# A planned instruction list for RWKV attention and a two-layer PReLU product: another way to pick the list, small reciprocals for the tables of powers, and idle matmuls ahead of the first dense product

## The chip, the core and the metric

The kernel runs on one core of one Trainium2 chip. The metric is device time in microseconds (us), the median of the runs shown. In what follows PE is TensorE (PEld its weight loads), DVE is VectorE, ACT is ScalarE, POOL is GpSimd and SP is SyncE, which only issues DMA transfers here.

## What is computed

A recurrent attention with a state of 48 x 48 per head runs over 768 steps, for 4 batches and 8 heads; its result goes through two dense products with a PReLU between them.

```python
def _attn_ref(r, k, v, w, u):            # (4, 8, 768, 48), w and u (8, 48)
    state = np.zeros((B, H, D, D))
    for t in range(S):
        kt, vt, rt = (k[:, :, t], v[:, :, t], r[:, :, t])
        cur = np.einsum('bhd,bhe->bhde', u[None] * kt, vt)
        y[:, :, t] = np.einsum('bhd,bhde->bhe', rt, state + cur)
        state = w[None, :, :, None] * state + np.einsum('bhd,bhe->bhde', kt, vt)

def _moe_ref(x, w_in, w_out, alpha):     # x (3072, 384), w_in (384, 2048)
    h = x @ w_in
    g = np.maximum(h, 0.0) + alpha * np.minimum(h, 0.0)
    return g @ w_out
```

`w` lies between 0.85 and 0.95.

## The kernel before

The 768 steps are cut into six chunks `c` of 128, and the eight heads into four pairs `q`. For a chunk and a pair, `attention` scales r by powers of w (`raw<-raw,W`, L403) and k by their inverses, forms the scores A (L459, or L469 in chunk 0), adds a diagonal `cu` and masks them (`base`, L479 to L505), and multiplies by v (`out`, L531; `out_of_tokens`, L561). In chunk 0 the diagonal comes from `c_sum` (L418), four tiny matmuls on the product r times k (L411), each followed by an idle one. The result is split into a rounded part and a rest (`split`, L626 to L637), the pieces `xh` and `xl` of the dense input; small transfers `lower` (`x<-x`, L367) bring the rows of pair 0 into place. The state T is updated by k^T v (`state_product`, L585, and `state_of_tokens`, L574). For pair 3 of chunk 0 k is first scaled by `scale_k` on DVE (`kk<-kk,wtok`, L592).

`table(m)` makes, per pair, the powers of w from -64 to 64 (`W`): a scan gives the upper half (L297), and a reciprocal of 64 columns the lower half (L300).

The dense part has 16 slices `i` of 128 hidden columns per chunk. `m_in` (L860, in later chunks L813) forms hp, ACT and DVE form the rounded `gh` and the rest `gl` of the PReLU, and `m_out` (L902) adds to three accumulators. Each operand is a sum of two rounded parts, so three matmuls stand for one. The parts `wh` and `wl` of slice i are made once, by `weights`: a load of 768 KB (`wraw<-wall`, L323), then ACT (L345), DVE (L348), ACT (L352) and DVE (L355). `wh_87` and `wl_103` are the parts of slice 0, `wh_88` and `wl_104` those of slice 1, and so on; in the changed kernel all these numbers are one higher.

Every operation is recorded as a `Piece` with an engine, an assumed duration and its dependences. `Plan.in_order` plans the pieces twelve times, forward with urgencies and backward for new ones (`forward`, `backward`), keeps the list whose planned end is earliest, and the program is written in the order of its planned starts. Each engine then runs its own part of the list strictly in order. So this one list sets the order on PE, DVE, ACT, POOL and SP. SP has eight transfers in flight at most. Where the plan has a gap on PE before the first `m_out`, the program writes idle matmuls (`warm`, L986: 128x256 on a tile `busy` of zeros) into it; 26 more stand at the very start.

Of the kernel before, what the change touches and what calls it, by code (L numbers as in the profile page):

```python
# [2 lines left out]

# [13 lines left out]
AF = mybir.ActivationFunctionType  # L17
ALU = mybir.AluOpType
# [9 lines left out]
MLAG = 3  # L28
# [9 lines left out]
DMA_RATE = 275.0  # L38

OVERLAP = {"DVE": 0.08, "ACT": 0.1}  # L40
ROUNDS = 12


class Buf:
# [31 lines left out]
class Plan:  # L76
# [1 line left out]


    def __init__(self):  # L80
        self.pieces, self.groups, self.log = [], {}, {}

    def buf(self, make, group=None, bufs=0):
        b = Buf(make, group, bufs)
# [4 lines left out]
    def add(self, eng, us, fn, r=(), w=(), rank=0.0, kb=0.0):  # L89
        p = Piece(eng, us, fn, r, w, rank, kb)  # L90
        for ref, wr in p.uses:
            b, part = ref if isinstance(ref, tuple) else (ref, None)
            if isinstance(b, Half):
                b, part = b.buf, (b.j, part)
            log = self.log.setdefault(b, [])
            for other, opart, owr in log:
                if other is not p and ((wr or owr) and (part is None or opart is None or part == opart)
                                       or b.bank and other.eng != p.eng and "PE" not in (other.eng, p.eng)):
                    p.after.add(other)
            log.append((p, part, wr))  # L100
        self.pieces.append(p)
        return p

    def in_order(self):
        for bs in self.groups.values():
            bs[:] = [b for b in bs if b in self.log]
            for n, b in enumerate(bs):
                users = [p for p, _, _ in self.log[b]]
                for p in users:
                    if n >= b.bufs:  # L110
                        p.after.update(q for q, _, _ in self.log[bs[n - b.bufs]])
                    if n:
                        p.behind.add(self.log[bs[n - 1]][0][0])
                    p.behind.add(users[0])
        number = {p: i for i, p in enumerate(self.pieces)}
        for p in self.pieces:
            p.behind.discard(p)
        best = None
        urgency = {p: p.rank for p in self.pieces}
        for n in range(ROUNDS):  # L120
            order = self.forward(urgency, number)
            end = max(p.end for p in order)
            if best is None or end < best[0]:
                best = end, {p: (p.start, p.end) for p in order}
            urgency = self.backward(number)
        for p, (start, end) in best[1].items():
            p.start, p.end = start, end
        return sorted(self.pieces, key=lambda p: (p.start, number[p]))

    def run(self, need, ready, key):  # L130

# [26 lines left out]
    def forward(self, urgency, number):  # L158
        def ready(p):
            return max([q.end + q.lag + (0.0 if q.eng == p.eng else 0.2 if q.eng == "PE" else 0.1) for q in p.after]  # L160
                       + [q.start + 0.001 for q in p.behind] + [0.0])

        dma, done = 0.0, []
        for p, start in self.run({p: p.after | p.behind for p in self.pieces}, ready,
                                 lambda p: (urgency[p], number[p])):
            p.start, p.end = start, start + p.us
            if p.eng == "SP":
                dma = max(dma, p.end + 1.5) + p.kb / DMA_RATE
                p.end = dma + 0.5
                self.landed.append(p.end)  # L170
            done.append(p)
        return done

    def backward(self, number):

        heirs, followers = {p: set() for p in self.pieces}, {p: set() for p in self.pieces}
        for p in self.pieces:
            for q in p.after:
                heirs[q].add(p)
            for q in p.behind:  # L180
                followers[q].add(p)
        ends, starts, dma = {}, {}, 0.0

        def ready(p):
            t = [starts[q] + p.lag + p.early + (0.0 if q.eng == p.eng else 0.2 if p.eng == "PE" else 0.1) for q in heirs[p]]
            t += [starts[q] + 0.001 - p.us for q in followers[p]]
            t = max(t + [0.0])
            return max(t, dma) + 1.8 + p.kb / DMA_RATE if p.eng == "SP" else t

        was = {p: p.start + p.us for p in self.pieces}  # L190
# [10 lines left out]
def rwkv_prelu_kernel(ctx: ExitStack, tc, rk, vkr, wP, uP, u, wall, alpha, w, r_all, k_all, v_all, oT):  # L201
    nc = tc.nc
# [7 lines left out]
    P = H // 2  # L210
    NB, NM = C * P, C * NF
    plan = Plan()
    add = plan.add
# [26 lines left out]
    T = [fixed([112, B, D], f"T{m}") for m in range(P)]  # L240

    uw = fixed([112, P, 2], "uw")
    wh, wl = ([fixed([128, 2 * NK, 128], f"{n}{i}", F32R) for i in range(NF)] for n in ("wh", "wl"))
    flag = fixed([1, 1], "flag", I32)
    busy = fixed([128, 256], "busy", mybir.dt.bfloat16)
# [9 lines left out]
    for t, dram in ((wp, wP), (up, uP)):  # L255
# [7 lines left out]
        rank=-100)  # L263
# [3 lines left out]
        r=[ones], w=[ident], rank=-100)  # L267
# [3 lines left out]
        w=[ones], rank=-100)  # L271
# [19 lines left out]
    for g in range(2):  # L291
        add("POOL", 0.25, lambda g=g: nc.gpsimd.tensor_tensor(
            out=uw()[half(g), :, g], in0=up()[half(g)], in1=wp()[half(g)], op=ALU.mult),
            r=[up, wp], w=[uw], rank=-97)
    def table(m):
        t, a = W[m], wp
        add("DVE", 0.3, lambda: nc.vector.tensor_tensor_scan(  # L297
            out=t()[:, 64:129], data0=a()[:, m:m + 1].broadcast_to([112, 65]), data1=unit(), initial=0.0,
            op0=ALU.mult, op1=ALU.add), r=[wp, unit], w=[t], rank=10 * m - 95)
        add("DVE", 0.55, lambda: nc.vector.reciprocal(t()[:, 0:64], t()[:, 128:64:-1]), w=[t], rank=10 * m - 95)  # L300
        add("POOL", 0.55, lambda: nc.gpsimd.tensor_tensor(
            out=w128()[:, m:m + 1], in0=t()[:, 128:129], in1=t()[:, 128:129], op=ALU.mult), r=[t], w=[(w128, m)],
            rank=10 * m - 85)
# [880 lines left out]
```

## Time and profile before

| | us |
|---|---|
| three runs | 491.72, 491.02, 489.53 (median 491.02) |
| the profiled execution | 490.89 |
| its span, first to last instruction | 489.0 |
| PE busy | 479.3 (98%) |
| DVE busy | 364.1 (74%) |
| ACT busy | 245.7 (50%) |
| POOL busy | 73.0 (15%) |

The profiled execution's own time is 1.89 us more than its span. In a busy time the ends of matmuls are modelled, so a busy PE is one that has been given work, not one at its peak; idle matmuls count as busy.

### The profile page before, as it was taken

How to read it: one execution, taken by the hardware profiler on the slowest of the kernel's cores; microseconds unless marked ns; L12 is line 12 of the kernel's file. 1: busy time of each engine (PE TensorE's matmuls, PEld its weight loads, DVE VectorE, ACT ScalarE, POOL GpSimd, SP SyncE). 2: the span in 40 equal slices, each digit the busy share in tenths (PEclk: the TensorE clock that was granted, in tenths of full speed). 3: DMA queues.
4: the chain of work that ended last, by engine and by line, in shares of the span. 5: the costliest groups of instructions: out<-in, count | busy, mean ns of one | idle time of the engine just before them, and what ended most of it. 6: DMA issues, size and time to landing. Idle time of an engine off the chain costs nothing.

```text
span 489.0 us, 10992 instructions
## 1 busy us (share of the span) xinstructions
PE 479.3 (98%) x4431; PEld 397.0 (81%) x4431; DVE 364.1 (74%) x658; ACT 245.7 (50%) x579; POOL 73.0 (15%) x76
## 2 busy tenths in 40 slices
PE   9999999999999999999999999999999999999996
PEld 7767877888888887887888888887888888888885
DVE  6989999899967897887897686686785745445542
ACT  1786776666654454543455554343753323532322
POOL 7416040041010132210210121030000000000000
PEclk9999999999999999999999999999999999999999
DMA  8894779640232633441122341120220000100001
GB/s 241 269 296 136 250 182 277 214 153 2 97 115 75 200 86 100 137 104 52 52 87 87 118 104 52 36 87 1 71 67 1 1 0 1 64 1 0 2 1 70
DMA packets 24600, 47.58 MB, mean 97 GB/s; under 512 B 3552, under 2 KB 12256, under 8 KB 24544
## 3 DMA queue, kind: packets, MB, share of 16 engines
q1 hardware_dynamic: 24000, 46.55, 31.5%
q8 instruction: 37, 0.61, 0.5%
q10 hardware_dynamic: 544, 0.27, 0.2%
q14 instruction: 19, 0.16, 0.1%
HBM read 38.15 MB, written 6.29 MB: 91 GB/s over the span
## 4 chain that ended last, share of the span: by engine, by line
PE 87%; ACT 5%; DVE 4%; DMA 1%; issue 1%; POOL 0%; SPq 0%; DVEq 0%; ACTq 0%
PE acc L902 36%; PE hp L860 19%; PE hp L813 18%; PE A L459 3%; PE y L539 2%; PE y L561 2%; PE hp L986 2%; ACT x L626 2%; DMA x<-x 1%; PE A L902 1%; PE hp L561 1%; ACT base L491 1%; PE y L574 1%; ACT g L825 1%; PE hp L574 1%
## 5 line engine op out<-in xcount | busy, mean ns | idle before, releaser
L860 PE MATMUL hp<-x,wh 128*128 128x512 f32 x288 | 98.3, 398 | 1.0 <-PE y L634 0.8
L902 PE MATMUL acc<-gh,wh 128*128 128x512 f32 (+1 forms) x282 | 79.8, 391 | 1.0 <-ACT gh L849 1.0
L902 PE MATMUL acc<-gh,wl 128*128 128x512 f32 (+1 forms) x282 | 79.7, 390 | 0.0
L902 PE MATMUL acc<-gl,wh 128*128 128x512 f32 (+1 forms) x282 | 79.2, 389 | 0.0
L844 DVE TENSOR_TENSOR g<-hp,g 128x512 f32<-128x512 f32 x48 | 32.7, 688 | 58.6 <-PE hp L813 30.7
L860 PEld LDWEIGHTS hp<-x,wh 128*128 128x128 f32 x288 | 54.0, 188 | 14.4 <-PE y L634 1.1
L849 ACT ACTIVATE gh<-g 128x512 fp32r<-128x512 f32 x48 | 30.2, 632 | 70.7 <-DVE g L846 62.2
L813 PE MATMUL hp<-x,wh 128*128 128x256 f32 (+1 forms) x192 | 62.4, 347 | 0.0
L825 ACT ACTIVATE g<-hp 128x256 f32<-128x256 f32 x96 | 34.4, 380 | 55.4 <-PE hp L813 55.0
L434 POOL TENSOR_TENSOR rr<-rr,kk 128x384 f32<-128x384 f32 x20 | 25.6, 1278 | 235.2 <-DMA kk<-vkr 140.7
L902 PEld LDWEIGHTS acc<-gl,wh 128*128 128x128 f32 x282 | 51.5, 188 | 10.9
L902 PEld LDWEIGHTS acc<-gh,wh 128*128 128x128 f32 x282 | 50.6, 188 | 11.7 <-ACT gh L849 1.4
L902 PEld LDWEIGHTS acc<-gh,wl 128*128 128x128 f32 x282 | 51.1, 188 | 10.6
L860 PE MATMUL hp<-x,wl 128*128 128x512 f32 x144 | 57.1, 397 | 1.0 <-issue 0.5
L867 DVE SCALAR_TENSOR_TENSOR g<-hp,alph,g 128x512 f32<-128x512 f32 x48 | 35.9, 747 | 18.5 <-ACT g L866 18.4
L866 ACT ACTIVATE g<-hp 128x512 f32<-128x512 f32 x48 | 28.6, 596 | 33.1 <-PE hp L860 32.8
L871 DVE TENSOR_TENSOR gl<-g,gh 128x512 fp32r<-128x512 f32 x48 | 36.1, 753 | 9.7 <-ACT gh L870 5.8
L813 PEld LDWEIGHTS hp<-x,wh 128*128 128x128 f32 x192 | 36.1, 188 | 7.0 <-ACT g L825 3.1
L870 ACT ACTIVATE gh<-g 128x512 fp32r<-128x512 f32 x48 | 30.1, 628 | 20.2 <-DVE g L867 18.3
L403 DVE TENSOR_TENSOR raw<-raw,W 112x512 f32<-112x512 f32 x45 | 39.5, 892 | 0.6 <-DMA raw<-rk 0.5
L491 ACT ACTIVATE base<-eye,cu 128x64 f32<-128x64 f32 x144 | 38.7, 337 | 0.8 <-DVE cu L442 0.8
L850 DVE TENSOR_TENSOR gl<-g,gh 128x512 fp32r<-128x512 f32 x48 | 32.8, 689 | 7.6 <-ACT gh L849 4.0
(184 smaller groups left out, 877.9 us busy)
## 6 DMA issues: line engine op xcount, KB each, us to landing
wraw<-wall SPq DMA_DIRECT2D x16, 767.8 KB, 5.3
raw<-rk SPq DMA_DIRECT2D x45, 224.0 KB, 3.5
v<-vkr SPq DMA_DIRECT2D x24, 192.0 KB, 4.0
kk<-vkr SPq DMA_DIRECT2D x21, 192.0 KB, 3.5
rr<-vkr SPq DMA_DIRECT2D x20, 192.0 KB, 2.5
oT<-o SPq DMA_DIRECT2D x12, 256.0 KB, 2.5
x<-x SPq DMA_DIRECT2D x36, 64.0 KB, 2.8
oT<-g SPq DMA_DIRECT2D x5, 256.0 KB, 2.3
```

The source lines that it names most:

```text
L403: add("DVE", 0.72 if c < 2 else 0.85, lambda t=t, tab=tab: nc.vector.tensor_tensor(out=t(), in0=t(), in1=tab().broadcast_to([112, B, L]), ...
L491: add("ACT", 0.39 if first else 0.34, lambda g=g, b=b: nc.scalar.activation(base[g]()[:, b], (ident if first else eye)(), AF.Copy, scale=c ...
L813: nc.tensor.matmul(bank()[:, cols], ws[a], xs[b], start=start and j == 0, stop=stop and j == 2, skip_group_check=True)
L825: add("ACT", 0.37, lambda: nc.scalar.activation(t()[:, cols], bank()[:, src], AF.Copy), r=[bank], w=[(t, part)], rank=rank - 100).early = 0.3
L844: add("DVE", 0.75, lambda g=g, bank=bank: nc.vector.tensor_tensor(out=g(), in0=bank(), in1=g(), op=ALU.add), r=[bank], w=[g], rank=m - 100)
L849: add("ACT", 0.64, lambda g=g, gh=gh: nc.scalar.activation(gh(), g(), AF.Copy), r=[g], w=[gh], rank=m - 100)
L850: add("DVE", 0.73, lambda g=g, gh=gh, gl=gl: nc.vector.tensor_tensor(out=gl(), in0=g(), in1=gh(), op=ALU.subtract), r=[g, gh], w=[gl], ran ...
L860: nc.tensor.matmul(hp(), a[i]()[:, k], x[c]()[:, k], start=(k == 0 and j == 0), stop=(k == NK - 1 and j == 2))
L867: add("DVE", 0.75, lambda: nc.vector.scalar_tensor_tensor(out=g(), in0=hp(), scalar=alph()[:, i:i + 1], in1=g(), op0=ALU.mult, op1=ALU.max ...
L870: add("ACT", 0.64, lambda: nc.scalar.activation(gh(), g(), AF.Copy), r=[g], w=[gh], rank=n - 100)
L871: add("DVE", 0.73, lambda: nc.vector.tensor_tensor(out=gl(), in0=g(), in1=gh(), op=ALU.subtract), r=[g, gh], w=[gl], rank=n - 99)
L902: nc.tensor.matmul(bank(), a[i]()[:, NK + k], x()[:, cols], start=(begin and j == 0), stop=(end and j == 2), skip_group_check=(c == C - 1))
```

## The change

There are three edits. First, `in_order` now plans from several starts: for each of five assumed delays of the loads (0 to 2 us, which `forward` adds to loads that start between 4 and 35 us), once from the ranks and once from the best list so far with random noise. Each list is then replayed in its fixed order (`replay`) with five delays, and the one whose mean end is earliest is kept; to a replayed end some us are added for each PE gap of over 0.9 us between 8 and 40 us. Second, the lower half of `W` is now the upper half times one reciprocal per row: a reciprocal of one column on DVE, and a multiplication, on DVE for table 0 and on ACT for tables 1 to 3. Third, idle matmuls may now stand directly ahead of the first dense product as well.

```diff
-ROUNDS = 12
+STARTS, SEED = 2,4
+ROUNDS, ASSUMED, LATE = 12, (0.0, 0.5, 1.0, 1.5, 2.0), (0.0, 0.5, 1.0, 1.5, 2.0)
...
-        best = None
-        urgency = {p: p.rank for p in self.pieces}
-        for n in range(ROUNDS):
-            order = self.forward(urgency, number)
-            end = max(p.end for p in order)
-            if best is None or end < best[0]:
-                best = end, {p: (p.start, p.end) for p in order}
-            urgency = self.backward(number)
+        best, draw = None, random.Random(SEED)
+        for again, self.late in enumerate(ASSUMED * STARTS):
+            spread = 0.0 if again < len(ASSUMED) else 0.4
+            urgency = {p: (best[1][p][0] if spread else p.rank) + draw.gauss(0.0, spread) for p in self.pieces}
+            for n in range(ROUNDS):
+                order = self.forward(urgency, number)
+                times = {p: (p.start, p.end) for p in order}
+                order = sorted(self.pieces, key=lambda p: (p.start, number[p]))
+                end = sum(self.replay(order, times, late) for late in LATE) / len(LATE)
+                if best is None or end < best[0]:
+                    best = end, times
+                urgency = self.backward(number, times)
...
+    def replay(self, order, times, late, show=False):
...
+                if last is not None and t - last - gap > 0.9 and 8.0 < t < 40.0:
+                    stood += min(2.5, 2.5 * (t - last - gap - 0.9) / 0.3)
...
+                end[p] = dma + 0.5 + late * (4.0 < t < 35.0)
...
-        add("DVE", 0.55, lambda: nc.vector.reciprocal(t()[:, 0:64], t()[:, 128:64:-1]), w=[t], rank=10 * m - 95)
+        add("DVE", 0.12, lambda: nc.vector.reciprocal(inverse()[:, m:m + 1], t()[:, 128:129]), r=[t], w=[(inverse, m)],
+            rank=10 * m - 95)
+        if m < 1:
+            add("DVE", 0.15, lambda: nc.vector.tensor_scalar(
+                t()[:, 0:64], t()[:, 64:128], inverse()[:, m:m + 1], None, op0=ALU.mult), r=[(inverse, m)], w=[t],
+                rank=10 * m - 95)
+        else:
+            add("ACT", 0.25, lambda: nc.scalar.activation(
+                t()[:, 0:64], t()[:, 64:128], AF.Copy, scale=inverse()[:, m:m + 1]), r=[(inverse, m)], w=[t],
+                rank=10 * m - 95)
...
-            hp_taken |= p.rank >= 0 and p.us == 0.704
             if hp_taken and not ready:
                 gap = 0
+            hp_taken |= p.rank >= 0 and p.us == 0.704
```

The list itself moves at many places in its first fifth and at few after that. Three places follow; the names are those of the two programs, without the numbers of the rows.

The first place is DVE at the start, up to the scaling of pair 1 (`raw<-raw,W_76`); before:

```order
L297 SCALAR_TENSOR_TENSOR W_75<-wp,unit 112x65
L297 SCALAR_TENSOR_TENSOR W_76<-wp,unit 112x65
L300 RECIPROCAL W_75<-W_75 112x64
L300 RECIPROCAL W_76<-W_76 112x64
L403 TENSOR_TENSOR raw<-raw,W_75 112x512 x2
L403 TENSOR_TENSOR raw<-raw,W_76 112x512
L411 TENSOR_TENSOR g<-raw 112x512
```

and in the changed kernel:

```order
L340 SCALAR_TENSOR_TENSOR W_75<-wp,unit 112x65
L340 SCALAR_TENSOR_TENSOR W_76<-wp,unit 112x65
L343 RECIPROCAL inverse<-W_75 112x1
L340 SCALAR_TENSOR_TENSOR W_77<-wp,unit 112x65
L346 TENSOR_SCALAR W_75<-W_75,inverse 112x64
L343 RECIPROCAL inverse<-W_77 112x1
L343 RECIPROCAL inverse<-W_76 112x1
L455 TENSOR_TENSOR raw<-raw,W_75 112x512 x2
L455 TENSOR_TENSOR raw<-raw,W_76 112x512 x2
L463 TENSOR_TENSOR g<-raw 112x512
```

Two reciprocals of 64 columns gave way to three of one column and one multiplication, the scan of table 2 came forward, and all four scalings now stand ahead of the first product r times k (L411 before, L463 now).

The second place is PE between the two halves of the first dense work: `A` are the scores of chunk 1, `acc<-v,kk` is the state product of pair 3 (L585 before, L637 now). Before, it stood behind the first two dense slices:

```order
L860 MATMUL hp<-x,wh_88 128x512
L860 MATMUL hp<-x,wl_104 128x512
L860 MATMUL hp<-x,wh_88 128x512 x2
L860 MATMUL hp<-x,wl_104 128x512
L860 MATMUL hp<-x,wh_88 128x512
L585 MATMUL acc_598<-v,kk 64x48
```

and now, behind the scores and eight idle matmuls of which the last is shown:

```order
L1038 MATMUL acc_522<-busy 128x256
L637 MATMUL acc_568<-v,kk 64x48
...
L912 MATMUL hp<-x,wh_88 128x512
L912 MATMUL hp<-x,wl_104 128x512
L912 MATMUL hp<-x,wh_88 128x512
L912 MATMUL hp<-x,wh_89 128x512
L912 MATMUL hp<-x,wl_105 128x512
```

The state product moved ahead of two thirds of both slices, which now take turns; behind them 14 idle matmuls stand ahead of slice 2.

The third place is DVE around the parts of the weights of slice 4 (`wl_107` before, `wl_108` now):

```order
L348 SCALAR_TENSOR_TENSOR wraw<-wraw,wx 128x768
L442 TENSOR_REDUCE cu<-rr 128x8
L871 TENSOR_TENSOR gl<-g,gh 128x512
L592 TENSOR_TENSOR kk<-kk,wtok 128x384
L355 SCALAR_TENSOR_TENSOR wl_107<-wraw,wh_91 128x768
```

and now:

```order
L400 SCALAR_TENSOR_TENSOR wraw<-wraw,wx 128x768
L923 TENSOR_TENSOR gl<-g,gh 128x512
L407 SCALAR_TENSOR_TENSOR wl_108<-wraw,wh_92 128x768
L548 COPY_PREDICATED base<-strict_70,A_532 128x256
```

Three operations stood between the two steps of these weights, and one stands there now.

## Rows read from the trace of the kernel before

**Rows 1.** The page: span, PE's and granted-clock rows of the summary.

```profile
span 489.0 us, 10992 instructions
PE 479.3 (98%) x4431; PEld 397.0 (81%) x4431; DVE 364.1 (74%) x658; ACT 245.7 (50%) x579; POOL 73.0 (15%) x76
...
PEclk9999999999999999999999999999999999999999
```

**Rows 2.** Busy time by stretch: stretch, its length, busy us (instructions) by engine.

```profile
0.00:40.00 40.00, 37.40 (x387) 29.47 (x388) 33.08 (x51) 22.45 (x45) 19.65 (x37) 1.00 0.86 260
62.00:100.00 38.00, 37.29 (x461) 29.73 (x460) 36.12 (x64) 26.84 (x50) 8.41 (x5) 1.00 0.73 214
484.00:489.00 5.00, 0.50 (x5) 0.29 (x3) 0.42 (x1) 0.21 (x1) 0.00 (x0) 0.92 0.34 118
```

**Rows 3.** Waits of PE over the whole span: total us, times, longest.

```profile
PE hp L986 <- DVE busy L287: 1.1, 1, 1.1
PE acc L902 <- ACT gh L849: 1.0, 1, 1.0
PE hp L860 <- PE y L634: 0.8, 1, 0.8
PE hp L860 <- issue: 0.5, 1, 0.5
PE hp L860 <- DVE wl L355: 0.4, 1, 0.4
PE acc L585 <- ACT wh L352: 0.3, 1, 0.3
PE hp L860 <- DMA x<-x: 0.2, 1, 0.2
```

**Rows 4.** Timeline of PE: start, us, what (idle before it).

```profile
1.13 6.25 PE L986 MATMUL hp<-busy 128*128 128x256 bf16 x30 [1.13 <-DVE busy L287]
...
8.41 0.38 PE L418 MATMUL acc<-uw,g 112*128 112x2 f32 x2
...
9.60 1.16 PE L469 MATMUL acc<-raw 48*128 48x128 f32 x16
...
25.07 0.47 PE L860 MATMUL hp<-x,wh 128*128 128x512 f32 x1 [0.78 <-PE y L634]
...
31.38 1.48 PE L986 MATMUL acc<-busy 128*128 128x256 bf16 x12
...
36.40 0.64 PE L585 MATMUL acc<-v,kk 128*64 128x48 f32 x16 [0.28 <-ACT wh L352]
```

**Rows 5.** Timeline of DVE, five stretches.

```profile
3.95 0.48 DVE L297 TENSOR_TENSOR_SCAN W<-wp,unit 112x65 f32<-112x65 f32 x2 [2.67 <-DMA wp<-wP]
4.34 0.94 DVE L300 RECIPROCAL W<-W 112x64 f32<-112x64 f32 x2
5.20 1.83 DVE L403 TENSOR_TENSOR raw<-raw,W 112x512 f32<-112x512 f32 x3
...
13.31 1.00 DVE L411 TENSOR_TENSOR g<-raw,gl 112x512 f32<-112x512 f32 x1
...
34.91 1.38 DVE L592 TENSOR_TENSOR kk<-kk,wtok 128x384 f32<-128x384 f32 x1
...
47.12 1.36 DVE L355 SCALAR_TENSOR_TENSOR wl<-wraw,wh 128x768 fp32r<-128x768 f32 x1
...
50.99 0.55 DVE L592 TENSOR_TENSOR kk<-kk,wtok 128x384 f32<-128x384 f32 x1
...
331.61 0.68 DVE L844 TENSOR_TENSOR g<-hp,g 128x512 f32<-128x512 f32 x1
```

**Rows 6.** Timeline of POOL, at the first of the two `kk` scalings.

```profile
34.42 1.46 POOL L434 TENSOR_TENSOR rr<-rr,kk 128x384 f32<-128x384 f32 x1 [10.68 <-DMA kk<-vkr]
```

**Rows 7.** Timeline of ACT, near the start.

```profile
8.59 0.20 ACT L262 ACTIVATE one<-one 128x1 f32<-128x1 f32 x1 [5.24 <-POOL one L261]
```

**Rows 8.** The chain that ended last, 25 to 34 us: start, us, what.

```profile
26.41 6.59 DMA x<-x
33.05 0.97 PE hp L860 x3
```

More of the change, by code (lines that the diff above doesn't have):

```diff
@@ L1 @@
 import heapq
+import random
 from contextlib import ExitStack
@@ L80, in __init__ @@
     def __init__(self):
-        self.pieces, self.groups, self.log = [], {}, {}
+        self.pieces, self.groups, self.log, self.late = [], {}, {}, 0.0
     def buf(self, make, group=None, bufs=0):
@@ L117, in in_order @@
             p.behind.discard(p)
-        best = None
-        urgency = {p: p.rank for p in self.pieces}
-        for n in range(ROUNDS):
-            order = self.forward(urgency, number)
-            end = max(p.end for p in order)
-            if best is None or end < best[0]:
-                best = end, {p: (p.start, p.end) for p in order}
-            urgency = self.backward(number)
+        best, draw = None, random.Random(SEED)
[10 more added lines that the diff above has]
+                urgency = self.backward(number, times)
+        self.late = 0.0
         for p, (start, end) in best[1].items():
@@ L128, in in_order @@
         return sorted(self.pieces, key=lambda p: (p.start, number[p]))
+    def replay(self, order, times, late, show=False):
+        free, landed, dma, last, stood = {}, [], 0.0, None, 0.0
+        start, end = {}, {}
+        filled, planned = False, None
+        for p in order:
+            t = free.get(p.eng, 0.0)
+            for q in p.after:
+                t = max(t, end[q] + q.lag + (0.0 if q.eng == p.eng else 0.2 if q.eng == "PE" else 0.1))
+            for q in p.behind:
+                t = max(t, start[q] + 0.001)
+            if p.eng == "PE":
+                gap = 0.0 if planned is None else max(0.0, times[p][0] - planned - 0.05)
+                planned = times[p][0] + p.us + p.more
+                if filled:
+                    t = max(t, last + gap)
+                    filled = not (p.us == 0.704 and p.rank == MLAG - 0.5)
+                if last is not None and t - last - gap > 0.9 and 8.0 < t < 40.0:
+                    stood += min(2.5, 2.5 * (t - last - gap - 0.9) / 0.3)
+                filled |= last is None
+                last = t + p.us + p.more
+            start[p], end[p] = t, t + p.us
+            free[p.eng] = t + p.us - OVERLAP.get(p.eng, 0.0)
+            if p.takes:
+                free["DVE"] = max(free.get("DVE", 0.0), t) + p.takes
+            if p.eng == "SP":
+                dma = max(dma, t + p.us + 1.5) + p.kb / DMA_RATE
+                end[p] = dma + 0.5 + late * (4.0 < t < 35.0)
+                landed.append(end[p])
+                if len(landed) >= 8:
+                    free["SP"] = max(free["SP"], landed[-8])
+        if show:
+            return max(end.values()), stood
+        return max(end.values()) + stood
     def run(self, need, ready, key):
@@ L168, in forward @@
                 dma = max(dma, p.end + 1.5) + p.kb / DMA_RATE
-                p.end = dma + 0.5
+                p.end = dma + 0.5 + self.late * (4.0 < p.start < 35.0)
                 self.landed.append(p.end)
@@ L172, in forward, with backward @@
         return done
-    def backward(self, number):
+    def backward(self, number, times):
         heirs, followers = {p: set() for p in self.pieces}, {p: set() for p in self.pieces}
@@ L188, in ready @@
             return max(t, dma) + 1.8 + p.kb / DMA_RATE if p.eng == "SP" else t
-        was = {p: p.start + p.us for p in self.pieces}
+        was = {p: times[p][0] + p.us for p in self.pieces}
         for p, at in self.run({p: heirs[p] | followers[p] for p in self.pieces}, ready,
@@ L242, in rwkv_prelu_kernel @@
     uw = fixed([112, P, 2], "uw")
+    inverse = fixed([112, P], "inverse")
     wh, wl = ([fixed([128, 2 * NK, 128], f"{n}{i}", F32R) for i in range(NF)] for n in ("wh", "wl"))
```

## The prediction

> **What bounds the kernel now.** I read the page first. PE is busy for 479.3 of 489.0 us, and its clock row reads full speed, 2.4 GHz, in every slice [rows 1]. So PE bounds the kernel, but two things hide in "busy". One is idle matmuls: the list before has 82 of them, 30 in one run at the start that takes 6.25 us [rows 4]. The other is the 9.7 us in which PE did nothing, and the table by stretch says where: 1.13 us before its first matmul [rows 3, 4], and 5.00 - 0.50 = 4.5 us behind its last, when the results are copied and stored [rows 2]. That leaves 9.7 - 1.1 - 4.5 = 4.1 us of real gaps: 2.6 - 1.1 = 1.5 in the first 40 us, 0.7 between 62 and 100 us [rows 2], 1.0 near 331 us, where `acc` waits for `gh`, and some 0.9 spread. The list of PE's waits names the longest: 0.8, 0.2, 0.3 and 0.4 us around the first dense slices, 0.5 later, and that 1.0 [rows 3].
>
> PE's useful matmuls are the same in both programs. So the change can give at most the 4.1 us of gaps plus what it saves in idle matmuls, and it can cost whatever new gaps the new order makes. In the first 40 us DVE is busy for 33.1 us [rows 2], strictly in order, so what PE waits for there is mostly DVE's place in the list.
>
> The measurement can tell about 0.5% from no change, 2.5 us here.
>
> **The start.** The list now has 26 idle matmuls at the start and 55 later, where it had 30 and 52. The 30 took 6.25 us, 0.21 each; twelve later ones took 1.48, 0.12 each [rows 4]. Four fewer at the start are 4 x 0.21 = 0.83 us, if PE's next operands are there by then; three more later cost 3 x 0.12 = 0.37.
>
> Are they there? Before, DVE began at 3.95 with two scans (0.24 each), two reciprocals (0.47 each), and the first scalings at 5.20, 0.61 each [rows 5]. Now three scans, three reciprocals of one column and one multiplication stand ahead of them: 3.95 + 3 x 0.24 = 4.67 plus four small operations. No row prices these. From above, each is at most the 0.47 of the large reciprocal, from below nothing; a 65-column scan, the nearest row, takes 0.24 and a one-column operation less, so I take 0.1. The first scaling then begins at 5.07, two are done at 6.3, and PE, free at 1.13 + 26 x 0.21 = 6.5, goes on at once: -0.83 us. At 0.24 they are done at 6.85 and PE gains 0.5; at 0.47 at 7.8, and PE starts 0.4 later than before. Net of the 0.37: **-0.46**, bounds -0.46 and +0.8.
>
> The multiplications for tables 1 to 3 went to ACT, which sat idle for 5.24 us ahead of 8.59 [rows 7]; table 1 is wanted two scalings (1.2 us) after table 0, so ACT's work lies beside DVE's. Without that cover, each would cost up to 0.47. Over the whole start DVE sheds about 4 x 0.47 - 5 x 0.1 = 1.4 us. That is worth nothing by itself, since PE ends the kernel and DVE doesn't; it makes PE's operands earlier, and counts only where PE waits, below. The planner's replay runs on the host and costs the chip nothing.
>
> **Gaps that go.** First, 0.78 us ahead of the first dense matmul at 25.07 [rows 4]: three idle matmuls, a state product and a masked product now stand there instead, real work in the main. Second, 0.2 us for `x<-x` at 33.05: that transfer was issued at 26.41 and took 6.59 us [rows 8], behind a 768 KB load and two of 224 KB; in the new list of SP it stands ahead of the next such load, behind two of 192 KB. Third, 0.28 us before L585 at 36.40 [rows 4]; the waits name ACT `wh`, but `scale_k` on DVE ended at 34.91 + 1.38 = 36.29 [rows 5], so that was it. Fourth, 0.4 us for `wl` of slice 4, made at 47.12 to 48.48 [rows 5]: three operations stood between its two DVE steps, now one. Together **-1.7**; the bound on the other side is 0, if each is only moved.
>
> **Gaps that come.** (a) The three `c_sum` of pairs 0 to 2 now follow each other on PE. One takes 9.60 - 8.41 = 1.2 us [rows 4]. DVE puts a scaling (0.61), a scan (0.24) and a product ahead of the third; a product takes about one scaling's time, or 1.00 when POOL is at work [rows 5]: 1.5 to 1.85 us. PE runs dry for 0.3 to 0.65 us; I take 0.5. (b) L585 of pair 3 now comes after the scores and eight idle matmuls, ahead of two thirds of the first two slices, and those, the 14 idle matmuls and slice 2 are queued behind it. It waits for `scale_k`, which on DVE stands behind the two splits of pair 3, and next to POOL's products of r and k. Beside such a product (34.42, 1.46 us [rows 6]) it took 1.38 us, without one 0.55 [rows 5]. So the gap is nothing at best and 0.28 + (1.38 - 0.55) = 1.1 us at worst; I take 0.4. Together **+0.9**, bounds 0 and +1.8.
>
> The Trainium skill (SBUF — State Buffer, "SBUF: two separate sides") says that VectorE, with two operands from SBUF, and GpSimd take their shared port in turn, the loser standing still for the whole instruction. The 1.38 against 0.55 us agree. By that rule a POOL product of 1.46 us [rows 6] that began just ahead would hold `scale_k` for all of it, and the gap (b) would be up to 0.28 + 1.46 = 1.7 us, the sum 0.6 higher at the worst end.
>
> **Later.** From slice 9 on the two lists differ only by single blocks of three or six matmuls that change places. Near 331 us six matmuls of `hp` now go ahead of the `acc` that waited; but they need a bank of `hp`, which DVE frees at 331.61 + 0.68 = 332.3 [rows 5], and PE went on at about the same time. I count 0 (bound -0.7, the six matmuls). Of the 0.7 us between 62 and 100 us I count **-0.2**, since weights come a little earlier (bounds -0.7 and 0).
>
> **The sum.** -0.46 - 1.7 + 0.9 - 0.2 = -1.46. The profiled execution took 490.89 us, 0.13 under the median of 491.02, so **489.4 us**.
>
> **Rivals.** *All the gaps go.* DVE's 1.4 us carry through, PE finds its operands each time: -0.46 - 1.7 - 0.7 for 62 to 100 us, and none to 0.7 near 331: 487.3 to 488.0. For it speaks that weights, `x<-x` and `wl` all move forward; against it, that (b) puts PE behind a longer chain of DVE and ACT.
>
> *The gaps only move.* PE's work is the same and the idle matmuls number 81 instead of 82; if 1.5 us of new gaps replace the 1.7, the time is 490.89 - 0.46 - 0.2 = 490.2 to 491. This is the case in which the new choice of list does nothing on the chip. For it speaks that the plan's own durations, not the chip's, still set the order.
>
> *PE falls back to its slow pace* (slower). The first idle matmuls went at 0.21 us each and later ones at 0.12 [rows 4]: PE begins at the lower level's pace, 256 columns in 0.21 us being 1.2 GHz, though the clock row reads full throughout [rows 1]. If `scale_k` or `x<-x` leaves PE dry around L585, between 27 and 32 us, it could fall back. A second start-up run would cost, for 26 matmuls' time, 26 x (0.21 - 0.12) = 2.3 us; with a gap of 2 us ahead of it, and none of the dense gaps filled: 490.89 - 0.46 + 2 + 2.3 = 494.7, or 493 with the other gaps gone. It decides from 2.5 us of loss, so the dry stretch and the fall must come together. Against it: no gap before was over 1.1 us, and 55 idle matmuls remain in the way.
>
> The Trainium skill (TensorE: Matmul & The Clock Gate, "What's actually happening" and "Why this matters for your kernels") says that PE's default is half rate, which activity lifts and an idle stretch brings back. The slow first run agrees; no row here shows a second fall.
>
> **How the numbers follow.** The forecast 0.40 (488.6 to 490.2), all gaps go 0.29, gaps move 0.20, the slow pace or a like loss 0.11. The predicted time is the likeliest's. The case of all gaps ends at 487.3, which I round down to 487.2 for the low end; the bounds of the small operations and of (b) together, +0.8 and +1.8 with nothing else gained, give 490.89 + 2.6 = 493.5, but not both at once in 8 of 10, so I end the range at 492.5. Faster by over 0.5% means under 488.6: the second case and a corner of the first, 0.31. Slower means over 493.5: 0.09, most of the last case. Within: 0.60.
>
> **What would show it.** After: the first scores start at 6.5 to 6.6 us, and the first scaling at about 5.1. The waits of PE lose the 0.8 and the 0.4, and show L585 (now L637) or nothing above 1.1. The third `c_sum` starts with a gap of about half a microsecond. The scores of the second pair of chunk 1 and all later work come 1 to 2 us earlier, and the tail stays 4.5 us. Wrong would be: a gap of over 1.5 us before 50 us, idle matmuls of 0.21 us after the start, or a span that moves by much more than PE's gaps and idle matmuls together.

## The result, and the profile after

The changed kernel takes 486.59 us (median of six runs, 485.75 to 487.63), the kernel before 490.79 beside it: a ratio of 0.9913, 95% interval 0.9890 to 0.9936. It is 4.2 us faster. The forecast was 489.4 with a low end of 487.2, so the direction was right and the gain almost three times what I counted.

The page of the profiled execution (486.39 us) answers to [rows 1]: span, busy time, granted clock.

```profile
span 484.4 us, 10994 instructions
PE 476.1 (98%) x4430; PEld 397.1 (82%) x4430; DVE 357.8 (74%) x659; ACT 247.4 (51%) x582; POOL 71.6 (15%) x76
...
PEclk9999999999999999999999999999999999999999
```

Of the 4.6 us of span, PE's busy time gives 3.2 and its idle time 1.4. DVE's busy time fell by 6.3 us, far more than the 1.4 that the tables take off it: e2 below, the new list with the old tables, is at 358.5 us, against 357.8 here. The stretches that answer to [rows 2], and one more:

```profile
0.00:40.00 40.00, 36.78 (x392) 29.70 (x393) 31.32 (x55) 24.87 (x53) 20.53 (x39) 1.00 0.92 268
62.00:100.00 38.00, 37.82 (x401) 30.66 (x393) 36.28 (x62) 27.15 (x50) 7.66 (x5) 1.00 0.72 223
300.00:400.00 100.00, 99.82 (x871) 83.80 (x870) 69.29 (x129) 45.03 (x118) 8.41 (x6) 1.00 0.11 33
480.00:484.40 4.40, 0.00 (x0) 0.00 (x0) 0.41 (x1) 0.00 (x0) 0.00 (x0) 0.74 0.38 132
```

PE idles more than before in the first 40 us (3.22 us against 2.60), and only 0.18 us from 62 to 100 and 0.18 from 300 to 400. The end is as it was. PE's waits, which answer to [rows 3]:

```profile
PE hp L1038 <- DVE busy L330: 1.1, 1, 1.1
PE A L521 <- DVE raw L455: 0.5, 1, 0.5
PE y L686 <- ACT x L678: 0.3, 1, 0.3
PE acc L637 <- DVE kk L644: 0.3, 1, 0.3
PE acc L521 <- DVE raw L455: 0.3, 1, 0.3
```

Every wait of [rows 3] but the first and L585's (now L637, 0.3) is gone, the 1.0 near 331 us too; what came is 0.5 at most, and all of it lies ahead of 31 us. PE's timeline (start, us, idle before it), which answers to [rows 4]:

```profile
1.13 4.54 PE L1038 MATMUL hp<-busy 128*128 128x256 bf16 x26 [1.13 <-DVE busy L330]
6.12 1.16 PE L521 MATMUL A<-raw 48*128 48x128 f32 x16 [0.45 <-DVE raw L455]
7.61 1.16 PE L521 MATMUL acc<-raw 48*128 48x128 f32 x16 [0.33 <-DVE raw L455]
...
10.90 0.35 PE L470 MATMUL acc<-uw,g 112*128 112x2 f32 x2
...
26.72 0.48 PE L912 MATMUL hp<-x,wh 128*128 128x512 f32 x1
...
30.84 0.67 PE L637 MATMUL acc<-v,kk 128*64 128x48 f32 x16 [0.34 <-DVE kk L644]
...
48.61 0.31 PE L591 MATMUL y<-raw,T 48*48 48x128 f32 x1
```

The last row is a landmark that the rest of this text uses: the first state block of chunk 1 (`y<-raw,T`, L539 before, L591 now). In both programs the same 347 useful matmuls stand ahead of it. The profile of the kernel before has it at 50.60, so PE was 2.0 us ahead here. From there to the last matmul it took 433.6 us before and 431.1 now: the other 2.6. And DVE, which answers to [rows 5]:

```profile
3.82 0.48 DVE L340 TENSOR_TENSOR_SCAN W<-wp,unit 112x65 f32<-112x65 f32 x2 [2.54 <-DMA wp<-wP]
4.21 0.14 DVE L343 RECIPROCAL inverse<-W 112x1 f32<-112x1 f32 x1
...
4.46 0.23 DVE L346 TENSOR_SCALAR W<-W,inverse 112x64 f32<-112x64 f32 x1
...
4.74 2.82 DVE L455 TENSOR_TENSOR raw<-raw,W 112x512 f32<-112x512 f32 x4
...
30.22 0.56 DVE L644 TENSOR_TENSOR kk<-kk,wtok 128x384 f32<-128x384 f32 x1
...
44.33 0.96 DVE L407 SCALAR_TENSOR_TENSOR wl<-wraw,wh 128x768 fp32r<-128x768 f32 x1 [0.37 <-ACT wh L404]
```

`wl` of slice 4 is done at 45.3 instead of 48.5.

### The profile page after: what moved, and what is told of

Read it like the earlier page. It is cut to its first block, busy times and chain, and to the rows that moved or that the text cites. A ratio compares the mean times of both kernels' runs of the same rounds, so it can differ in the third digit from the quotient of the medians.

```text
span 484.4 us, 10994 instructions
## 1 busy us (share of the span) xinstructions
PE 476.1 (98%) x4430; PEld 397.1 (82%) x4430; DVE 357.8 (74%) x659; ACT 247.4 (51%) x582; POOL 71.6 (15%) x76
## 4 chain that ended last, share of the span: by engine, by line
PE 91%; DMA 4%; ACT 3%; DVE 0%; issue 0%; ACTq 0%; SPq 0%
PE acc L954 39%; PE hp L912 21%; PE hp L865 19%; PE A L511 3%; PE y L591 2%; DMA wraw<-wall 2%; PE y L613 2%; DMA v<-vkr 1%; ACT x L678 1%; PE A L954 1%; PE hp L613 1%; DMA up<-uP 1%; PE y L626 1%; PE hp L626 1%; PE acc L963 1%; ACT base L543 1%
## 5 line engine op out<-in xcount | busy, mean ns | idle before, releaser
L486 POOL TENSOR_TENSOR rr<-rr,kk 128x384 f32<-128x384 f32 x20 | 26.6, 1328 | 227.1 <-DMA kk<-vkr 131.0
L954 PEld LDWEIGHTS acc<-gh,wh 128*128 128x128 f32 x282 | 50.8, 188 | 9.8
L455 DVE TENSOR_TENSOR raw<-raw,W 112x512 f32<-112x512 f32 x45 | 36.1, 815 | 1.0 <-DMA raw<-rk 0.8
```

The costliest lines, as they stand in the source:

```text
L455: add("DVE", 0.72 if c < 2 else 0.85, lambda t=t, tab=tab: nc.vector.tensor_tensor(out=t(), in0=t(), in1=tab().broadcast_to([112, B, L]), ...
L954: nc.tensor.matmul(bank(), a[i]()[:, NK + k], x()[:, cols], start=(begin and j == 0), stop=(end and j == 2), skip_group_check=(c == C - 1))
```

## The experiments

The list is a table of numbers, so it can be written out and given to either program. All experiments but e8, e12 and e13 have this edit, in the kernel before or the changed one; what differs is the list that `listed` returns (`old` and `new` below), with the idle matmuls that belonged to each place. The small diffs below say in words what changes in that table of numbers.

```diff
-    order = plan.in_order()
-    fill, last, hp_taken, ready = {}, None, False, False
...
+    number, idle_ahead = listed()
+    order = [plan.pieces[n] for n in number]
+    fill = dict(zip(order, idle_ahead))
```

Theory A: the list made the gain. Theory B: the lighter start of DVE, which my sum put first. Theory C: single stalls that come by chance. Theory D, added later: the list stands late loads. Of the third edit no experiment with the new list is needed: that list has no planned gap ahead of the first dense product, and without the edit the program comes out the same, instruction by instruction.

**e1, the tables alone** (the changed kernel, old list).

```diff
-listed = new
+listed = old
```

> The list and the idle matmuls of the kernel before, written out as they stood, with the new tables (a reciprocal of one column each, the multiplication on DVE for table 0 and on ACT for 1 to 3, each at the place of its old reciprocal). Theory A, the list made the gain: PE is held by its 30 idle matmuls until 7.3 us in any case, so the earlier tables are worth 0 to 0.4 us: 490.4 to 490.8. Theory B, DVE's lighter start made it (1.4 us less work there, which goes on into all that waits for DVE): 488.5 to 489.5. Theory C, chance: part of the gain is single stalls (0.7 at 84 us, 1.1 at 331 us in the execution profiled before) that an execution has or has not, whatever the list: any value within 1.5 of 490.8, and those two stalls may be missing here.

490.18 us against 489.97 of the kernel before on the same chip, ratio 1.0004 (0.9984 to 1.0024). No gain of the tables by themselves can be told (from 0.8 us of gain to 1.2 of loss by the interval), which speaks against theory B; e13 and e14 below test it again.

**e2, the list alone** (the kernel before, new list).

```diff
-listed = old
+listed = new
```

> The list and the idle matmuls of the changed kernel, written out, with the old tables (reciprocals of 64 columns on DVE, nothing on ACT). DVE has to do three scans and three reciprocals of 0.47 ahead of the first scaling: it begins at about 5.9 instead of 4.74 us and PE's first scores at 7.3 instead of 6.1. Theory A: that 1.2 us is lost and the rest of the gain stays: 487.8. Theory B: most of the gain goes: 489.5 to 490.5. Theory C: as A, plus or minus up to 1.5 by stalls later on, which would show as PE waits of over 0.4 us behind 60 us at other places than before.

485.94, ratio 0.9920 (0.9897 to 0.9943): all of the gain. The start went as expected, the first scaling at 5.79 and PE's first scores at 7.09 us, a whole microsecond behind the changed kernel's, and nothing of it was left at the landmark:

```profile
7.09 1.16 PE L469 MATMUL A<-raw 48*128 48x128 f32 x16 [0.91 <-DVE raw L403]
...
48.37 0.31 PE L539 MATMUL y<-raw,T 48*48 48x128 f32 x1
```

So what is won ahead of 7 us is given back by waits behind it. **e13 and e14** are the changed kernel and e2 once more, on one chip.

> The changed kernel as it is: 486.6, within 0.5, and of e14 within 0.7 if the tables are worth nothing beside the list; 0.5 to 1.2 under e14 if DVE's lighter start counts.

> The new list with the old tables, as in e2: within 0.7 of e13 if the tables are worth nothing beside the list; 0.5 to 1.2 above e13 if DVE's lighter start counts; under e13 by 0.5 if the small operations and ACT's multiplications cost more than they save.

486.65 and 486.29, ratios to before 0.9938 (0.9915 to 0.9961) and 0.9934 (0.9911 to 0.9957): no difference. Theory A holds: the list makes the gain, with either tables.

**e3 and e4, the list cut at 50 us** (`head` holds what the first list plans to start ahead of 50 us; e3 on the changed kernel, e4 on the kernel before).

```diff
+e3 = [p for p in new if p in head] + [p for p in old if p not in head]
+e4 = [p for p in old if p in head] + [p for p in new if p not in head]
```

> The changed kernel's tables and its list up to the planned time of 50 us, and behind it the old list. PE was 2.0 us ahead at about 50 us, the other 2.6 of the span came later (1.2 between 62 and 100, 1.2 near 331 us). Theory A, the new order of the later blocks removed those stalls: they come back here, 489.0. Theory C, they were chance or follow from the head (weights that come earlier): they stay away in part, 486.6 to 488, and the profile shows no wait of 1.0 us of acc for gh near 327 us.

> The old tables and the old list up to the planned time of 50 us, and behind it the new list. Theory A: the later 2.6 us are gained, 488.2 to 488.5. Theory C: the later stalls do not depend on the order of the blocks; 489.5 to 490.8, and the profile shows one of them again or another of that size.

e3 took 486.83, ratio 0.9932 (0.9908 to 0.9956); e4 488.47, ratio 0.9965 (0.9949 to 0.9981). Each part gains, 3.1 and 1.5 us; together that is 4.6 beside the 4.0 (e2) to 4.2 of the whole, no difference that the measurement can tell. e3 lies in theory C's range and not in A's, so more than I had expected follows from the head; e4 lies where theory A put it. The stretches that count are 62 to 100 and 300 to 400 us; e1 has the old order in all of it, and here are e1, e3 and e4:

```profile
62.00:100.00 38.00, 37.40 (x460) 29.61 (x460) 36.67 (x63) 26.99 (x50) 7.68 (x5) 1.00 0.71 216
300.00:400.00 100.00, 99.14 (x968) 83.21 (x968) 70.68 (x131) 45.86 (x121) 7.22 (x6) 1.00 0.13 39
```

```profile
62.00:100.00 38.00, 37.82 (x385) 30.40 (x375) 36.13 (x64) 26.27 (x50) 7.79 (x5) 1.00 0.75 228
300.00:400.00 100.00, 99.09 (x868) 82.93 (x867) 69.24 (x127) 44.62 (x119) 6.83 (x6) 1.00 0.11 34
```

```profile
62.00:100.00 38.00, 37.73 (x463) 30.35 (x462) 36.20 (x64) 26.88 (x50) 6.32 (x4) 1.00 0.77 225
300.00:400.00 100.00, 99.82 (x973) 84.17 (x969) 70.05 (x131) 47.03 (x123) 8.98 (x6) 1.00 0.13 39
```

The idle time between 300 and 400 us, 0.86 in e1, goes with the new order there (e4) and not with the new head (e3, 0.91). PE's stall in 62 to 100 us goes with the new head (0.60 to 0.18, though the rest is old) and mostly with the new rest as well. Theory C is left with one piece: the 0.46 us at 84 us for which the profile of before names no releaser was not seen again in four more executions of the old list (another such wait, of 1.4 us, stands in e15 below).

What stops PE near 331 us is DVE, and POOL beside it. e1, then e4, DVE's timeline and POOL's first products there:

```profile
326.45 0.69 DVE L830 TENSOR_TENSOR base<-o 128x256 f32<-128x256 f32 x1
327.07 1.50 DVE L455 TENSOR_TENSOR raw<-raw,W 112x512 f32<-112x512 f32 x1
...
328.82 1.50 DVE L455 TENSOR_TENSOR raw<-raw,W 112x512 f32<-112x512 f32 x1
...
325.85 1.01 POOL L486 TENSOR_TENSOR rr<-rr,kk 128x384 f32<-128x384 f32 x1 [19.21 <-DMA kk<-vkr]
326.94 1.07 POOL L490 TENSOR_TENSOR rr<-rr,utab 128x384 f32<-128x384 f32 x1
```

```profile
326.01 0.41 DVE L778 TENSOR_TENSOR base<-o 128x256 f32<-128x256 f32 x1
326.34 0.68 DVE L403 TENSOR_TENSOR raw<-raw,W 112x512 f32<-112x512 f32 x1
...
327.28 0.68 DVE L403 TENSOR_TENSOR raw<-raw,W 112x512 f32<-112x512 f32 x1
...
325.68 3.16 POOL L434 TENSOR_TENSOR rr<-rr,kk 128x384 f32<-128x384 f32 x1 [19.13 <-DMA kk<-vkr]
```

With the old order DVE's two scalings take 1.50 us each and POOL's product 1.0; with the new one they take 0.68 and the product 3.16. The scalings took 1.50 in each of seven profiles with the old order there (before, e1, e3, e6, e10, e15, e16), and 0.68 in each of eight with the new one (after, e2, e4, e5, e7, e11, e13, e14), where POOL's product took 2.1 to 3.2. One program stands between: e9 below, the new order without idle matmuls, had one scaling at 0.68 and one at 1.50.

**e5, the new order behind 300 us alone** (kernel before, the same cut at 300).

```diff
-listed = old
+listed = [p for p in old if p in head300] + [p for p in new if p not in head300]
```

> The kernel before with the old list up to the planned time of 300 us and the new order of the blocks behind it. If the stall of acc for gh near 331 us belongs to the old order of the blocks (it was 1.0, 0.6 and 0.6 us in three executions with the old order there and missing in three with the new one), it is missing here and the time is 0.6 to 1.0 us under before. If it belongs to chance in what POOL and DVE do side by side there, it is seen again, or the time is that of before within 0.4.

490.75, ratio 1.0005 (0.9981 to 1.0030). The stall near 331 us was gone, and a new one of 0.8 us (hp for `g` of ACT) stood at some 302 us, at the seam of the two lists. So the new order takes the one stall away and here brings another; that this comes from what it was planned behind is argued, not tried.

**e6 and e7, one more load** ahead of the first weights, in the kernel before and in the changed one.

```diff
             p.fn()
+            if p is late:
+                nc.sync.dma_start(junk, rk[C - 1, 0])
```

> The kernel before with one more load (448 KB, of no use, issued by SP ahead of the first weights at about 10 us); it makes every load behind it later by about 1.7 us (448 KB at the 260 GB/s of the first 40 us). Theory D, the new list gains because it stands late loads: the old list pays most of it, plus 1 to 2 us; the waits for x<-x and for weights (hp for wl) before 50 us grow. Rival: the loads are not what PE waits for there, plus or minus 0.5.

> The changed kernel with the same load of no use at the same place. Theory D: its list was picked over loads that come up to 2 us late, so it pays under 0.7 us, and the distance between the two kernels grows from 4 to 5 us or more. Rival: both kernels pay the same, 0 to 2 us, and the distance stays 4.

490.52, ratio 1.0009 (0.9985 to 1.0033), and 487.28, ratio 0.9926 (0.9902 to 0.9949). The distance did not grow: this doesn't support theory D. But the test was weak. Against e5, which has the same order there, the loads behind the added one landed between 0.4 us earlier and 0.9 later, mostly some 0.5 later, and without any added load the same transfer lands up to 2 us apart from one execution to the next: the fourth load behind the first weights at 21.1, 22.4, 23.0 and 23.2 us in four executions of the old order.

**e8, picked without delays.**

```diff
-ROUNDS, ASSUMED, LATE = 12, (0.0, 0.5, 1.0, 1.5, 2.0), (0.0, 0.5, 1.0, 1.5, 2.0)
+ROUNDS, ASSUMED, LATE = 12, (0.0, 0.0, 0.0, 0.0, 0.0), (0.0,)
```

> The changed kernel whose list is picked again in ten starts of twelve rounds, but with no delay of the loads, neither in the planning nor in the replay. It is another list, with 70 idle matmuls instead of 81. Theory D: it waits for loads in the first 50 us as the old one did, 488.5 to 490.5, and its times spread over 3 us or more. Rival, more tries are what counts: 486 to 487.5, with a spread of about 2 us as in the changed kernel.

488.67 (487.60 to 490.41), ratio 0.9958 (0.9942 to 0.9974): inside the range of theory D, with a spread of 2.8 us. But its profile, its slowest execution, does not show what theory D says. Ahead of 50 us PE waits for no load and for no `wl`. Instead the granted clock falls (the column behind POOL: 0.97 from 0 to 50 us), and near 331 us stands the stall of the old order (the first wait below), with both scalings of DVE at 1.50. The stretch, and what PE waited for longest behind its first matmul:

```profile
0.00:50.00 50.00, 45.88 (x413) 36.07 (x414) 40.06 (x63) 31.00 (x65) 23.58 (x40) 0.97 0.77 235
...
PE acc L954 <- ACT gh L901: 0.7, 1, 0.7
PE A L364 <- DVE base L557: 0.6, 1, 0.6
PE acc L954 <- ACT gh L922: 0.6, 1, 0.6
PE acc L719 <- ACT cu L475: 0.5, 1, 0.5
```

**e12, another seed**, with the delays:

```diff
-STARTS, SEED = 2,4
+STARTS, SEED = 2,2
```

> The changed kernel with another seed of the noise (2 instead of 4), so with another list that was picked over the same delays. Replayed by the program's own planner it ends at 481.9 us without delay and at 483.5 with 2 us, the changed kernel's at 480.8 and 483.1, the list picked without delays at 482.0 and 486.0 (with 5 more for gaps), the old one at 483.3 and 487.5 (with 5 more). If what counts is that the list stands late loads, it comes close to the changed kernel, 486.8 to 487.8, and clearly under the one picked without delays (488.67). If the changed kernel's list was merely a lucky one, 488.5 to 490.5.

487.44 (486.88 to 487.83), ratio 0.9948 (0.9931 to 0.9966). Its median is 1.2 us under e8's, but on another chip: by the ratios to the kernel before, 0.9948 and 0.9958, the intervals overlap, so that the list picked over delays is again the better one is likely and not shown. In the profile it waits 1.2 us for one `x<-x` and otherwise hardly. The order of the four lists on the chip is that of the planner's own replays quoted above. The spread says the same: 97 runs of the kernel before beside these experiments lie between 488.0 and 493.8, 24 of the new list (with either tables) between 485.7 and 487.6. That is two lists of one kind and two of the other. The times agree with theory D, but they do not show its cause, for three more reasons. Replayed without any delay the four already stand in this order, so it does not single the delays out. In their profiles e8 idles 0.7 us more than e12 from 300 to 400 us, where PE waits for no load. And of the two it is e12 that waits for a load.

What speaks for theory D is another row: in each of the five profiles of the old list (before, e1, e5, e6, e16) PE waits ahead of 60 us for `x<-x` (0.2 to 1.3 us) and for `wl` (0.2 to 0.5), in none of the five of the new list for either. So the new list does stand the loads as they come; that choosing it over delays made it so isn't shown.

**e9, no idle matmuls in the gaps of the plan.**

```diff
-    fill = dict(zip(order, idle_ahead))
+    fill = dict.fromkeys(order, 0)
```

> The changed kernel's list written out, without the 37 idle matmuls that stand in the gaps of the plan; the 26 at the start, the 16 beside c_sum and the 2 later ones stay. If PE falls back to its slow pace where it is left dry (25 to 37 us), the dense matmuls behind step at more than 0.23 us and the time rises by 1.5 to 4 us. If not, the gaps simply stand open: PE idle in the profile grows by some 3 us, and the time is that of the changed kernel within 0.6, or up to 1 us less where PE was held by an idle matmul although its operands were there.

487.14 (485.99 to 489.82), ratio 0.9940 (0.9922 to 0.9957). The median is within 0.6 us of the changed kernel, as expected if the gaps simply stand open. The exception is the clock: over the whole run it was 0.996 or less in three of the seven, where none of 24 runs of the new list with its idle matmuls was under 0.997. The profiled execution was the slowest of the seven, and shows what the idle matmuls ward off (the column behind POOL is the granted clock):

```profile
25.00:30.00 5.00, 5.00 (x42) 3.87 (x42) 3.04 (x5) 3.46 (x8) 0.00 (x0) 0.66 0.98 286
...
40.00:45.00 5.00, 5.00 (x18) 3.94 (x17) 4.31 (x6) 4.29 (x10) 3.19 (x3) 0.74 0.42 126
...
40.44 1.48 PE L954 MATMUL acc<-gh,wh 128*128 128x512 f32 x3
```

The clock fell to half in both stretches, behind PE waits of 1.75 and 1.78 us, and three dense matmuls that take 0.86 us take 1.48. This is the third rival of the prediction, in a program without the cover.

**e10 and e11, the list cut at the first dense product** (26 and 24 us).

```diff
+e10 = [p for p in new if p in head26] + [p for p in old if p not in head26]
+e11 = [p for p in old if p in head24] + [p for p in new if p not in head24]
```

> The changed kernel's tables and its list up to the first dense product (planned time 26 us), the old list behind it. With the new list up to 50 us the time was 486.83, with the old one 490. If the order of the attention of chunk 0 made the gain of the head, 487 to 488. If the order behind the first dense product made it (the state product of pair 3 and the two slices that take turns, the earlier weights): 489 to 490, with waits of L637 for scale_k and of hp for wl as in the kernel before.

> The old tables and the old list up to the first dense product (planned time 24 us), the new list behind it: the mirror image. If the attention of chunk 0 made the gain of the head: 488 to 489.5 (the old list up to 50 us gave 488.47). If the order behind the first dense product made it: 486.5 to 487.5, with no wait of hp for wl between 44 and 72 us.

489.68, ratio 0.9995 (0.9974 to 1.0016), and 490.75, ratio 1.0016 (0.9997 to 1.0035): neither program gains. e10 lies in the range of its second case, e11 above both of its ranges. What e11 loses it loses ahead of the landmark, with PE's waits of 1.0 and 1.1 us for `kk` and a clock of 0.72 from 25 to 30 us; behind it PE is as quick as in the changed kernel (the table below), so the new rest keeps its gain there. e11's first 50 us:

```profile
0.00:50.00 50.00, 45.73 (x422) 36.63 (x423) 39.69 (x61) 27.52 (x57) 21.96 (x40) 0.97 0.77 230
```

Over the whole run the clock was 0.996 or less in nine of its twelve runs (median 490.75); the two with 1.000 took 489.0. So the clock goes with some 1.7 us of what e11 lost; no experiment kept it up there. In e10, behind the new start, the old rest sends PE into scores that still want a buffer:

```profile
28.70 0.44 PE L511 MATMUL A<-raw 48*64 48x128 f32 x4
30.72 1.04 PE L511 MATMUL A<-raw 48*64 48x128 f32 x28 [1.59 <-ACT wtok L367]
```

The granted clock was 0.66 in the 5 us behind. **e15** puts idle matmuls there.

```diff
-    fill[first scores of chunk 1] = 6
+    fill[first scores of chunk 1] = 20
```

> e10 with 14 more idle matmuls ahead of the scores of chunk 1 that left PE dry for 1.6 us. If the fall of the granted clock behind that stretch was what the part of the list lost (idle matmuls at 0.21 and more, a dense step of twice 0.23 us, 1.0 to 1.7 us in all), it does not fall here and the time is 1 to 1.7 us under e10: 488.0 to 488.7. If it was the stretch itself and the other waits: 489.4 to 490, and the wait only moves into the idle matmuls.

490.88, ratio 1.0018 (1.0001 to 1.0034). The clock stayed at 1.00 in the profile, and the time did not fall but lies above both ranges: other waits stood there (1.0 for `kk`, 0.7 for `x<-x`, and 1.4 with no releaser named between 62 and 100 us). PE reached the landmark at 51.6 us, for 50.8 in e10. So keeping the clock up did not bring e10's part its gain; for e11's part, e15 says nothing.

**e16, the third edit alone**, in the old list.

```diff
-    fill[first dense product] = 0
+    fill[first dense product] = 4
```

> The kernel before with the four idle matmuls that the third edit lets stand directly ahead of the first dense product (the plan of the old list has a gap of 0.5 us there, in which PE waited 0.8 us in the profile). They take 0.46 us of a wait that is there anyway: no difference, within 0.4 of before. If the clock falls there in some executions and they keep it up, 0.5 to 1 less; if they hold the dense product up when its operands come early, up to 0.5 more.

490.70, ratio 1.0012 (0.9993 to 1.0031): no gain. The median is 1.0 above that of before, outside my 0.4, but the interval includes no difference.

Where PE stood, in the profile of each: the landmark, the time from there to the last matmul, and PE's idle time in two stretches.

| list ahead of 50 us / behind | profiles | landmark | to the last matmul | idle 62:100 | idle 300:400 |
|---|---|---|---|---|---|
| old / old | before, e1, e6, e16 | 50.6 to 51.9 | 432.8 to 433.6 | 0.49 to 0.72 | 0.60 to 1.28 |
| new / new | after, e2, e7, e13, e14 | 48.4 to 49.1 | 430.9 to 431.4 | 0.18 to 0.25 | 0.18 to 0.19 |
| new / old | e3 | 48.2 | 432.0 | 0.18 | 0.91 |
| old / new | e4 | 52.6 | 431.3 | 0.27 | 0.18 |
| old / old, new behind 300 | e5 | 51.3 | 433.1 | 0.61 | 0.98 |
| new up to 26 / old | e10 | 50.8 | 432.5 | 0.49 | 0.59 |
| old up to 24 / new | e11 | 53.1 | 431.0 | 0.18 | 0.19 |
| another seed's list | e12 | 49.3 | 431.5 | 0.18 | 0.27 |

No version here beats the changed kernel by more than the measurement can tell; e2, with the old tables, is its equal.

## Why the prediction was wrong

**What failed is the step "Later".** I counted 0 for 331 us and -0.2 for 62 to 100 us; the two profiled executions differ by 2.6 us behind the landmark. Over all profiles of the two whole lists (the first two rows of the table) the means differ by 2.1 behind the landmark and by 2.5 ahead of it, where I had forecast -0.2 and -1.3; so the head was mis-sized too, by the less of the two. My reason at 331 us was that the six matmuls of `hp` need a bank which DVE frees at 332.3. That was read from a DVE that POOL had held up for over 2 us; in the new order DVE frees it in time, and PE's idle time from 300 to 400 us is 0.18 us. (PE's own blocks stand in another order there too, and the two were not separated.) A date that another engine's bad luck has set is no bound. For 62 to 100 us I bounded the gain by 0.7; e3 shows that the new head takes nearly all of it. That it does so by the earlier weights (`wl` of slice 4 at 45.3) is argued, not tried.

**A second error is in how I priced a stall.** I took the idle time in brackets. But the record of a 128x512 matmul is 0.39 us long where the next one starts 0.23 us behind it, so each stall costs some 0.16 us more than it shows as idle. The kernel before, PE's timeline:

```profile
69.81 0.39 PE L860 MATMUL hp<-x,wh 128*128 128x512 f32 x1
70.26 0.50 PE L860 MATMUL hp<-x,wl 128*128 128x512 f32 x1
...
84.23 0.51 PE L860 MATMUL hp<-x,wh 128*128 128x512 f32 x1
85.20 0.50 PE L860 MATMUL hp<-x,wl 128*128 128x512 f32 x1 [0.46 <-issue]
```

From 84.23 to 85.20 is 0.97, 0.74 more than a step, and the idle column says 0.46; from 69.81 to 70.26 a wait of 0.22 shows as no idle at all. So my cap of 4.1 us on what gaps can give was too low, and the four gaps that go were worth more than 1.7: by starts 0.94, 0.35, 0.44 and 0.58, which is 2.3.

**The start**, -0.46: the rows came as forecast or better (first scaling 4.74 for 5.07, first scores 6.12 for 6.5, the small operations 0.06 to 0.14 from start to start). Its worth was wrong. The 26 idle matmuls took 4.54 us, not 5.5, since PE came to its fast pace earlier in this execution; e2 started its scores 1 us later and lost nothing. By these runs the term is about 0, as far as can be told, and the tables with it (e1, e14). That DVE's 1.4 us are worth nothing by themselves was right.

**Gaps that go**, -1.7: all four went, and so did that at 62 to 72 us. **Gaps that come**, +0.9: L637 waits 0.34 here (I took 0.4; 0.3 to 0.9 in other executions of this list). The third `c_sum`, for which I took 0.5, stands at 10.90 with no idle shown; PE's new wait for DVE is 0.45 and 0.33 a little earlier, ahead of the first two scores. With 0.32, 0.34 and 0.18 between 21 and 26 us, which I had not seen, the new waits come to 2.0 us. Up to the landmark I had -1.3 in all, and got -2.0.

**The rivals.** *All the gaps go* (0.29) comes nearest: the gaps that it names went, though PE did not find its operands each time. Its price of 487.3 was too high for the two reasons above. *The gaps only move* is what e5 and e10 do, parts of the list, and not the whole. *PE falls back to its slow pace* did not occur, with a granted clock of 1.00 from 0 to 40 us, and e9, the same list without them, shows what the idle matmuls do for this list. Idle matmuls alone do not keep the clock up: in the profiles of e8, e10 and e11 it fell with 70, 79 and 87 of them in the list. Nor does the clock divide the two lists: it was 0.996 or less over the run in 8 of the 97 runs of the kernel before. By the Trainium skill (TensorE: Matmul & The Clock Gate, "What's actually happening") an idle stretch brings PE's half rate back; e9's rows agree.

## What to carry to other kernels

Where a fixed list sets the order on every engine, ask first whether each stall in the profile is a property of the work or of its place, and try the new list without the other edits and the old list with them: two runs told here that the arithmetic edits were worth nothing. Price a stall of pipelined matmuls from start to start, not by the idle column, and don't use as a bound a date that another engine reached late. A piece of a good list in another list can lose at the seam what it gains elsewhere: cut at 50 us both pieces kept their gains, cut at 24, 26 and 300 us the programs gained nothing. So judge the list whole, and over the spread of what varies from run to run; that picking it over assumed delays helps was not shown.

## What the runs showed of the hardware that I had not expected

PE's move to its fast pace is not a matter of the program alone. With the same start, full clock was granted from 3.9 to 6.9 us in different executions; 30 idle matmuls took 4.8 to 6.3 us accordingly, and 26 took 4.3 to 5.3.

Nor does the length of a wait alone say whether the clock falls later. In e8's profile it fell at 22.1 us behind waits of 0.5 and 0.6 us; in e7's PE waited 1.0 us for ACT and in e16's 1.3 for `x<-x`, and it was granted 1.00 throughout.

DVE and POOL at their shared port: the Trainium skill (SBUF — State Buffer, "SBUF: two separate sides") says that whichever instruction starts first gets it for its whole length. e1's rows agree. In e4 POOL's product began at 325.68, DVE's first operation at 326.01, and it is POOL that took 3.16 us while DVE ran four operations unhindered; by their recorded starts (rough on POOL) that is the other way round. Which of the two gives way followed the list in fifteen profiles, and e9 shows that it isn't the list alone. What in that order decides it stays open: it wasn't tried alone.
